# Finer loads, quartered scores, TensorE dummies and new step weights in the opening of a banded-attention and PReLU kernel

## The chip, the cores and the metric

The kernel runs on one core of one Trainium2 chip. The metric is the time of one execution on the device in microseconds (us). The core has a matrix engine, TensorE (PE in the profile, with its weight loads as PEld), three engines for elementwise work, VectorE (DVE), ScalarE (ACT) and GpSimd (POOL), and SyncE (SP), which here issues nearly all transfers between the device memory and the core's own memory. Every engine works through its own queue of instructions in a fixed order. TensorE writes its results into banks of an accumulator memory, which POOL's instructions in this kernel never touch.

## What is computed

The reference is attention over a sliding window of 64 positions, followed by a feed-forward layer whose activation is a PReLU with a slope per hidden unit (8 batches, 8 heads, 576 positions, head dimension 64; 4608 tokens, model width 512, hidden width 2048).

```python
scores = scale * np.matmul(q, k.transpose(0, 1, 3, 2))
rel = pos[:, None] - pos[None, :]
mask = (rel >= 0) & (rel < 64)
scores = np.where(mask, scores, -1000000000.0)
scores = scores - np.max(scores, axis=-1, keepdims=True)
attn = np.exp(scores)
attn = attn / (np.sum(attn, axis=-1, keepdims=True) + 1e-09)
x = np.matmul(attn, v)          # heads side by side: 4608 x 512
h = x @ w_in
g = np.maximum(h, 0.0) + alpha * np.minimum(h, 0.0)
out = (g @ w_out).astype(np.float32)
```

q, k and v are float32. The two weight matrices arrive as float64 and are taken apart inside the kernel.

## The kernel before

**Tiles.** The 4608 tokens are 36 tiles of 128. For a tile t the attention needs the queries of its two 64-position blocks and the keys and values of three blocks (its own two and the one before), with a window of 128 keys per query block. `q_load`, `k_load` and `v_load` bring them: q in one transfer of 256 KB, k in one of 384 KB (three blocks, into one of two buffers), v in two of 256 KB, each into 64 of the 128 partitions.

**Attention of a tile.** `a_score` multiplies q with k in 32 small products into two accumulator banks; the half x of the heads (even or odd head pair) has a bank each. `a_least` (DVE) adds the mask and takes the least negated score of a head, `a_exp` (ACT) the exponential with its sum, `a_sum` (ACT) adds the small constant, `a_inverse` (DVE) the reciprocal, `a_scale` (POOL) multiplies. `a_turn` transposes on PE with an identity matrix, four heads per bank, `a_turned` copies back (DVE for tiles 0 and 1, ACT after), and `a_value` multiplies with v in 32 small products. The result is split into a high part `xh` (ACT, `a_xh`) and a remainder `xl` (DVE, `a_xl`), so that two fast products stand for one exact one.

**Weights.** Each of 32 weight chunks c (even c of w_in, odd c of w_out) is a `raw` transfer of 512 KB, and runs through a chain: `tw` and `mn` (DVE) mask exponent and mantissa, `tx` (ACT) and for odd c `mx` (ACT, which puts a sign in), `ep` and `vl` (DVE) join the pieces, `pr` (POOL) multiplies, `hi` (ACT) rounds to the high part, `lo` (POOL) takes the remainder.

**Feed-forward.** A cell (n, f) is a block n of two or three tiles and a chunk f of 128 hidden units: 12 products into `h` (`m_hidden`: three pairs of high and low parts, four each), `m_slopes` (ACT) and `m_larger` (DVE) for the PReLU, `m_high` (ACT) for `gh`, `m_low` (POOL) for `gl`, and three products of 512 columns per tile into the output accumulator (`m_add`: gl with wout_h, gh with wout_l, gh with wout_h).

**Order.** The first nine tiles' attention, all weight chunks and the first three blocks (two tiles each) form the opening. `opening_graph` (L38) lists its steps with an engine, an assumed duration and what each takes and frees; `list_schedule` (L137) places them by rank (longest path plus a weight from `favour`), and the order that it draws is written out as the fixed order of each engine's queue. The names in the graph are those above: s scores, le, ex, sm, rc, sc softmax, tu transposes, td copy back, av values, xh, xl, h products, sl, la, gh, gl activation, o output products, ev and out eviction and store. A step name with `i.` ahead is the issue of a transfer. After the opening a plain loop follows (`cell`, `eighth`): one attention eighth after every few cells, with k and q of the next tile asked for at its first eighth, v at its last.

Of the kernel before, what the change touches and what calls it, by code (L numbers as in the profile page):

```python
# [18 lines left out]
RING = 6  # L19
# [6 lines left out]
WHOLE = (0, 1, 2)  # L26
# [4 lines left out]
class Op:  # L31
    def __init__(self, engine, busy, done, after, take, free):
        self.engine, self.busy, self.done = engine, busy, done
        self.after, self.take, self.free = after, take, free
        self.rank = 0.0


def opening_graph():  # L38
# [9 lines left out]
    def load(name, service, after=(), take=(), queue="SP"):  # L48
        op("i." + name, queue, 0.64, after, [take] * bool(take) + [("lane " + name, ["lane"])])
        op(name, "DMA", service, ["i." + name], free=["lane " + name])  # L50
# [6 lines left out]
    for t in range(EARLY + 1):  # L57
        done = [f"s.{t-2}.0", f"s.{t-2}.1"] if t > 1 else []
        load(f"q.{t}", 1.05, done, queue="ACT" if t == 0 else "SP")
        load(f"k.{t}", 1.6, done)  # L60
        for u in range(2):
            load(f"v.{t}.{u}", 1.05, [f"av.{t-2}"] if t > 1 else [])
    for c in range(2 * NCELL):
        load(f"raw.{c}", 2.0 if c % 2 else 2.2, take=(f"raw.{c}", ["raw"]))

    for t in attention:
        bank = ["po", "psa"] if t < 2 else ["psa"]
        score = [f"k.{t}", f"q.{t}"]
        score += ([f"s.{t-1}.0", f"s.{t-1}.1"] if t else []) + ([f"av.{t-2}"] if t > 1 else [])
        if t in WHOLE:  # L70
            op(f"s.{t}.0", "PE", 0.94, score, take=[(f"s.{t}.0", bank), (f"s.{t}.1", bank)])
            op(f"s.{t}.1", "PE", 0.0, [f"s.{t}.0"], done=0.0)
        for u in range(2):
            if t not in WHOLE:
                op(f"s.{t}.{u}", "PE", 0.87, score, take=(f"s.{t}.{u}", bank))
            for e in range(NH_PAIRS):
                g = u * NH_PAIRS + e
                op(f"le.{t}.{g}", "DVE", 0.21,
                   [f"s.{t}.{u}"] + ([f"tu.{t-2}.0", f"tu.{t-2}.1"] if t > 1 else []) + (["le.%d.0" % t] if g else []),
                   free=[f"s.{t}.{u}"] if e == NH_PAIRS - 1 else [], done=0.36)  # L80
                op(f"ex.{t}.{g}", "ACT", 0.39, [f"le.{t}.{g}"], done=0.6)
            op(f"sm.{t}.{u}", "ACT", 0.25, [f"ex.{t}.{u*NH_PAIRS+e}" for e in range(NH_PAIRS)], done=0.35)
# [3 lines left out]
            op(f"td.{t}.{u}", "ACT" if t > 1 else "DVE", 0.55 if t > 1 else 0.6,  # L86
               [f"tu.{t}.{u}"] + ([f"av.{t-2}"] if t > 1 else []), free=[f"tu.{t}.{u}"])
        op(f"av.{t}", "PE", 1.0, [f"td.{t}.0", f"td.{t}.1", f"v.{t}.0", f"v.{t}.1"]
           + ([f"h.{(t-RING)//2}.{last}"] if t >= RING else []), take=(f"av.{t}", bank))
# [23 lines left out]
    for n in range(3):  # L113
        pair = [2 * n, 2 * n + 1]
        for f in range(NCELL):
            before = [f"h.{n}.{f-1}"] if f else [f"h.{n-2}.{last}"] if n > 1 else []
            op(f"h.{n}.{f}", "PE", 1.44, [f"lo.{2*f}"] + [f"xl.{t}" for t in pair] + before,
               take=(f"h.{n}.{f}", ["ph"]))
            op(f"sl.{n}.{f}", "ACT", 0.39, [f"h.{n}.{f}", "ad"], take=(f"g.{n}.{f}", ["g"]))
# [17 lines left out]
def list_schedule(ops, slots, favour):  # L137


    names = list(ops)  # L140
    needs = {n: len(set(ops[n].after)) for n in names}
# [15 lines left out]
    for n in names:  # L157
        if not needs[n]:
            heappush(ready[ops[n].engine], (0.0 if ops[n].engine == "DMA" else -rank[n], n))
    order, begun, ends, now = [], {}, [], 0.0  # L160
    stir = set(ENGINES)
    while True:
        for e in ENGINES:
# [3 lines left out]
            while ready[e]:  # L167
                key = heappop(ready[e])
                n = key[1]
# [13 lines left out]
                heappush(ends, (now + o.busy, 0, n))  # L183
                heappush(ends, (now + o.done, 1, n))
# [7 lines left out]
        while ends and ends[0][0] <= now + 1e-9:  # L192
            _, landed, n = heappop(ends)
            if not landed:
# [5 lines left out]
            for m in then[n]:  # L200
                needs[m] -= 1
                if not needs[m]:
                    e = ops[m].engine
                    stir.add(e)
                    heappush(ready[e], (now if e == "DMA" else -rank[m], m))
    if len(order) < len(names):
        raise RuntimeError(str((now, left, [k for k, p in held.items() if p == "psa"][-6:], [n for n, _ in order[-40:]], {e: [k[1] for k in ready[e]][:8] for e in ENGINES})))
# [3 lines left out]
TILE_FAVOUR = [305, -52, 78, 372, -192, -315, -70, -391, 34, -311, -259]  # L211
BLOCK_FAVOUR = [539, 231, 26, -322]
KIND_FAVOUR = dict(
    ad=(187, -89), alpha=(6, -97), at=(-83, -32), av=(-85, 87), ep=(74, -136), ev=(86, 17), ex=(73, -346),
    gh=(-67, -185), gl=(200, 42), h=(-47, 98), hi=(71, 217), k=(142, -346), la=(-135, 6), le=(48, 49),
    lo=(68, -161), mn=(4, 37), mx=(140, 10), o=(-83, -90), out=(-109, 157), pr=(-10, -70), q=(180, 254),
    raw=(-11, 76), rc=(-89, 63), s=(-133, -145), sc=(-87, -25), sl=(92, -147), sm=(305, -95), td=(-67, 59),
    tu=(4, 120), tw=(-109, 125), tx=(117, 189), v=(-105, 115), vl=(103, -99), xh=(-25, -155),
    xl=(-104, 41),
# [3 lines left out]
def favour(name):  # L223
# [3 lines left out]
    fixed, slope = KIND_FAVOUR.get(kind, (0, 0))  # L227
    if kind in ("o", "ev", "out"):
        return BLOCK_FAVOUR[at[0] // 2] + fixed + slope * (at[1] / NCELL if kind == "o" else 1)
    if kind in ("h", "sl", "la", "gh", "gl"):  # L230
        return BLOCK_FAVOUR[at[0]] + fixed + slope * at[1] / NCELL
    if kind in ("raw", "tw", "tx", "mn", "mx", "ep", "vl", "pr", "hi", "lo"):
        return fixed + slope * at[0] / (2 * NCELL)
    if at:
        return TILE_FAVOUR[at[0]] + fixed + slope * at[0] / EARLY
    return fixed
# [3 lines left out]
def banded_attention_then_prelu_ffn(  # L240
# [41 lines left out]

    masks = const.tile([P, 3, KW], F32, name="masks")
# [42 lines left out]

    def fetch(c):
# [17 lines left out]
    def exponent(c):  # L345
        two = cv[c]["two"]
        nc.scalar.activation(two, two, AF.Relu, scale=8.0, bias=ebias if c % 2 else ebias20)
# [7 lines left out]
    def signed_mantissa(c):  # L355
        man = cv[c]["man"]
# [9 lines left out]
    def join(c):  # L366
        d = cv[c]
        d["val"] = val = io.tile([P, E], F32, tag="val", name=f"val_{c}", bufs=2)
        nc.vector.scalar_tensor_tensor(out=val, in0=d["low"],  # L369
                                       scalar=s52_sb[:, c // 2:c // 2 + 1] if c % 2 else 2.0**-32,  # L370
                                       in1=d["man"], op0=ALU.mult, op1=ALU.add)

    def product(c):
        d = cv[c]
        nc.gpsimd.tensor_tensor(out=d["val"], in0=d["val"], in1=d["exp"].bitcast(F32), op=ALU.mult)  # L375
# [8 lines left out]
    def high_part(c):  # L384
        val, hi, _ = parts(c)
        nc.scalar.copy(hi, val)

    def low_part(c):
        val, hi, lo = parts(c)
        nc.gpsimd.tensor_tensor(out=lo, in0=val, in1=hi.bitcast(F32), op=ALU.subtract)  # L390
# [7 lines left out]

    def of_tile(t, name, shape):
# [20 lines left out]
    def a_score(t, halves=(0, 1), banks=("psa", "psa")):  # L420
# [3 lines left out]
        k = d["k"].rearrange("p a (b h w) -> p a b h w", b=3, h=2)  # L424
        s = d.setdefault("s", {})
        for x, from_ in zip(halves, banks):
            s[x] = a_bank(f"s_{t}_{x}", from_)
        for a in range(2):
            for h in range(2):
                for u in range(2):  # L430
                    for x in halves:
                        r, us = slice(x * D, (x + 1) * D), slice(u * W, (u + 1) * W)
                        nc.tensor.matmul(s[x][us, 2 * a + h], q[r, a, h, us], k[r, a, u:u + 2, h, :],  # L433
# [24 lines left out]
    def a_sum(t, halves=(0, 1)):  # L458

        d = st[t]  # L460
        g = slice(halves[0] * NP, (halves[-1] + 1) * NP)
        nc.scalar.activation(d["sm"][:, g], d["sm"][:, g], AF.Identity, bias=eps)

    def a_inverse(t, halves=(0, 1)):
        d = st[t]
        g = slice(halves[0] * NP, (halves[-1] + 1) * NP)
        nc.vector.reciprocal(d["rc"][:, g], d["sm"][:, g])  # L467

    def a_scale(t, halves=(0, 1)):
        d = st[t]  # L470
        g = slice(halves[0] * NP, (halves[-1] + 1) * NP)
        w, rc = d["w"][:, g, :], d["rc"][:, g]
# [287 lines left out]
```

## Time and profile before

| | us |
|---|---|
| median of 3 runs (lowest, highest) | 934.24 (934.04, 935.03) |
| the profiled execution | 934.54 |
| its span | 932.8 |
| TensorE busy in the span | 912.3 |
| VectorE, ScalarE, GpSimd busy | 438.0, 430.5, 348.1 |

The span runs from the first to the last instruction of the program; the difference to the execution's own time lies around it. Rows of the profile name a line of the kernel (L433), the engine, the operation and the tiles as output<-input. A row of the timeline begins with start and duration; what stands in brackets is how long the engine was idle before and what ended that. A row of a group has the count, then busy time, mean duration of one in ns, and idle time before it with its causes. A wait row has total, times and longest.

### The profile page before, as it was taken

How to read it: one execution, taken by the hardware profiler on the slowest of the kernel's cores; microseconds unless marked ns; L12 is line 12 of the kernel's file. 1: busy time of each engine (PE TensorE's matmuls, PEld its weight loads, DVE VectorE, ACT ScalarE, POOL GpSimd, SP SyncE). 2: the span in 40 equal slices, each digit the busy share in tenths (PEclk: the TensorE clock that was granted, in tenths of full speed). 3: DMA queues.
4: the chain of work that ended last, by engine and by line, in shares of the span. 5: the costliest groups of instructions: out<-in, count | busy, mean ns of one | idle time of the engine just before them, and what ended most of it. 6: DMA issues, size and time to landing. Idle time of an engine off the chain costs nothing.

```text
span 932.8 us, 17053 instructions
## 1 busy us (share of the span) xinstructions
PE 912.3 (98%) x6601; PEld 812.3 (87%) x6601; DVE 438.0 (47%) x1329; ACT 430.5 (46%) x1204; POOL 348.1 (37%) x330
## 2 busy tenths in 40 slices
PE   4899999999999999999999999999999999999998
PEld 3688889888988888888889889888888888889997
DVE  5798981224544444444444444444443443443111
ACT  5887884454444434434444444444443443432322
POOL 3889994224222233333222232332322222222221
PEclk9999999999999999999999999999999999999999
DMA  9775641111322112211122112222112212100000
GB/s 254 212 207 176 192 147 46 52 54 45 102 52 85 51 52 66 55 51 52 52 53 85 51 52 86 51 52 85 52 51 55 83 51 52 57 1 1 34 1 34
DMA packets 55216, 69.78 MB, mean 75 GB/s; under 512 B 3408, under 2 KB 48480, under 8 KB 55136
## 3 DMA queue, kind: packets, MB, share of 16 engines
q1 hardware_dynamic: 54832, 68.43, 26.0%
q8 instruction: 52, 0.85, 0.4%
q10 hardware_dynamic: 304, 0.27, 0.1%
q14 instruction: 28, 0.23, 0.1%
HBM read 59.25 MB, written 9.44 MB: 74 GB/s over the span
## 4 chain that ended last, share of the span: by engine, by line
PE 94%; DVE 2%; POOL 2%; ACT 1%; DMA 1%; issue 0%; POOLq 0%; DVEq 0%
PE h L565 43%; PE o L608 42%; PE s L433 4%; PE av L507 4%; PE t L490 1%; ACT w L451 1%; POOL val L375 1%; DMA q<-qT 1%; POOL w L473 0%; POOL gl L594 0%; POOL wout_l L390 0%; POOL win_l L390 0%; DVE exp L363 0%; DVE val L369 0%; DVE two L342 0%
## 5 line engine op out<-in xcount | busy, mean ns | idle before, releaser
L594 POOL TENSOR_TENSOR gl<-g,gh 128x384 fp32r<-128x384 f32 (+1 forms) x208 | 197.3, 948 | 548.9 <-ACT gh L587 543.3
L580 DVE SCALAR_TENSOR_TENSOR g<-h,s_sb,g 128x384 f32<-128x384 f32 (+1 forms) x208 | 122.0, 587 | 336.4 <-ACT g L574 333.6
L574 ACT ACTIVATE g<-h,sa_sb 128x384 f32<-128x384 f32 (+1 forms) x208 | 115.6, 556 | 262.7 <-PE h L565 258.4
L608 PE MATMUL o<-wout_h,gl 128*128 128x512 f32 x576 | 227.6, 395 | 1.2 <-POOL gl L594 1.2
L608 PE MATMUL o<-wout_l,gh 128*128 128x512 f32 x576 | 226.9, 394 | 0.0
L608 PE MATMUL o<-wout_h,gh 128*128 128x512 f32 x576 | 224.2, 389 | 0.0
L565 PE MATMUL h<-xh,win_h 128*128 128x384 f32 (+1 forms) x832 | 174.2, 331 | 0.4 <-DVE g L580 0.3
L565 PE MATMUL h<-xl,win_h 128*128 128x384 f32 (+1 forms) x832 | 168.8, 324 | 0.0
L565 PE MATMUL h<-xh,win_l 128*128 128x384 f32 (+1 forms) x832 | 167.8, 323 | 0.0
L587 ACT CAST gh<-g 128x384 fp32r<-128x384 f32 (+1 forms) x208 | 101.6, 489 | 124.4 <-DVE g L580 118.6
L565 PEld LDWEIGHTS h<-xh,win_h 128*128 128x128 f32 x832 | 141.3, 188 | 18.8 <-issue 1.2
L485 DVE STREAM_TRANSPOSE pt<-w 32x256 f32<-32x256 f32 x324 | 141.2, 436 | 5.5
L565 PEld LDWEIGHTS h<-xl,win_h 128*128 128x128 f32 x832 | 142.4, 188 | 0.1
L565 PEld LDWEIGHTS h<-xh,win_l 128*128 128x128 f32 x832 | 139.6, 188 | 0.0
L608 PEld LDWEIGHTS o<-wout_h,gh 128*128 128x128 f32 x576 | 108.1, 188 | 24.2
L451 ACT ACTIVATE w<-w,nm 128x128 f32<-128x128 f32 x288 | 113.1, 396 | 28.0 <-DVE nm L444 27.7
L608 PEld LDWEIGHTS o<-wout_h,gl 128*128 128x128 f32 x576 | 108.1, 188 | 18.5 <-POOL gl L594 1.8
L608 PEld LDWEIGHTS o<-wout_l,gh 128*128 128x128 f32 x576 | 108.3, 188 | 13.5
L444 DVE CUSTOM_DVE_ANT_0 w<-s,masks 128x128 f32<-128x128 f32 x288 | 71.1, 285 | 15.6 <-PE s L433 15.3
L473 POOL TENSOR_TENSOR w<-w,rc 128x1024 f32<-128x1024 f32 (+1 forms) x45 | 70.0, 1558 | 18.8 <-DVE rc L467 18.8
L518 DVE TENSOR_TENSOR xl<-av,xh 128x512 fp32r<-128x512 f32 x36 | 24.9, 691 | 99.6 <-ACT xh L513 99.5
L433 PEld LDWEIGHTS s<-k,q 64*64 64x64 f32 x1152 | 39.4, 142 | 24.0 <-PE o L608 9.6
(46 smaller groups left out, 535.1 us busy)
## 6 DMA issues: line engine op xcount, KB each, us to landing
v<-vN SPq DMA_DIRECT2D x72, 256.0 KB, 4.2
k<-kT SPq DMA_DIRECT2D x36, 384.0 KB, 4.7
out<-os SPq DMA_DIRECT2D x36, 256.0 KB, 2.3
q<-qT SPq DMA_DIRECT2D x35, 256.0 KB, 4.3
raw<-w_in SPq DMA_DIRECT2D x16, 512.0 KB, 4.1
raw<-w_out SPq DMA_DIRECT2D x16, 512.0 KB, 3.6
q<-qT ACTq DMA_DIRECT2D x1, 256.0 KB, 5.2
alpha_rows<-alpha ACTq DMA_DIRECT2D x1, 8.0 KB, 5.0
```

The source lines that it names most:

```text
L433: nc.tensor.matmul(s[x][us, 2 * a + h], q[r, a, h, us], k[r, a, u:u + 2, h, :], start=True, stop=True)
L444: nc.vector.tensor_tensor_reduce(out=d["w"][:, g, :], in0=d["s"][u][:, e], in1=mask, op0=ALU.add, op1=ALU.min, scale=-SCALE, scalar=3.0e38 ...
L451: nc.scalar.activation(w, w, AF.Exp, scale=-1.0, bias=d["nm"][:, g:g + 1], accum_out=d["sm"][:, g:g + 1])
L473: nc.gpsimd.tensor_tensor(out=w, in0=w, in1=rc.unsqueeze(2).broadcast_to(list(w.shape)), op=ALU.mult)
L485: nc.vector.transpose(pt[ks, :, r], w[r, :, ks])
L507: nc.tensor.matmul(av[r, e, us], v[:, e, u, r], pt[:, g, us], start=True, stop=True)
L565: nc.tensor.matmul(ph[:, :nt], wt[:, c, fs], xt[:, c, xs], start=(k == 0), stop=(k == 3 * NP - 1))
L574: nc.scalar.activation(g, ph[:, :nt], AF.Copy, scale=sa_sb[:, f:f + 1])
L580: nc.vector.scalar_tensor_tensor(out=g, in0=ph[:, :nt], scalar=s_sb[:, f:f + 1], in1=g, op0=ALU.mult, op1=ALU.max)
L587: nc.scalar.copy(gh, gs[n, f])
L594: nc.gpsimd.tensor_tensor(out=gl, in0=g, in1=gh.bitcast(F32), op=ALU.subtract)
L608: nc.tensor.matmul(po[t], gt[:, ts], wt[:, f, :], start=(f == 0 and k == 0), stop=(f == NF - 1 and k == 2))
```

## The change

It has these parts; the first three hold for all 36 tiles and all cells, the others for the opening alone:

1. v is loaded in four transfers of 128 KB per tile, one for each head pair, each into all 128 partitions. The source pattern is written by hand: two overlapping pairs of blocks, 64 positions, 256 elements.
2. k lives in a ring of seven blocks over three tiles: the first tile of a round loads three blocks (384 KB), the other two load two (256 KB).
3. In `m_add` the three products come in the order gh with wout_h, gl with wout_h, gh with wout_l (also after the opening).
4. Tile 0's q and k are loaded in two parts each (a).
5. For tiles 0, 1, 5, 6, 7 and 8 the score step is cut by a, not by bank: a step fills two quarters of both banks, and the softmax, transposes and copies of a half go with it (`heads`, `of_half`).
6. The identity is made on POOL ahead of the masks, and 40 products of the identity with itself stand in PE's queue as dummies of lowest rank.
7. The first three cells' products of each opening block become three steps each, with needs of their own.
8. 43 steps move to DVE: 19 gl, 5 lo, 6 pr, 7 sc from POOL, 3 td and 3 xh from ACT; the copies td of tiles 0 and 1 go from DVE to ACT. For the one odd chunk whose lo moves, mx falls away and the sign comes in with hi and lo.
9. Assumed durations and the rank weights are new, so the fixed order of all queues in the opening is drawn anew.

```diff
+COUPLED = (0, 1, 5, 6, 7, 8)
+APART = (0,)
+WARM = 40
+FINE = 3
+KRING = 3
+MOVED = (
+    "gl.0.1", "gl.0.5", "gl.0.6", "gl.0.8", "gl.0.10", "gl.0.14", "gl.1.1", "gl.1.3", "gl.1.6", "gl.1.8",
+    "gl.1.9", "gl.1.13", "gl.1.15", "gl.2.0", "gl.2.6", "gl.2.7", "gl.2.9", "gl.2.11", "gl.2.13", "lo.4",
+    "lo.8", "lo.9", "lo.24", "lo.26", "pr.5", "pr.11", "pr.27", "pr.28", "pr.29", "pr.30", "sc.4.1",
+    "sc.5.0", "sc.6.0", "sc.6.1", "sc.7.0", "sc.7.1", "sc.8.1", "td.2.1", "td.7.0", "td.8.0", "xh.2",
+    "xh.6", "xh.7",
+)
...
+def heads(t, u):
+
+    if t in COUPLED:
+        return [2 * u, 2 * u + 1, NH_PAIRS + 2 * u, NH_PAIRS + 2 * u + 1]
+    return list(range(u * NH_PAIRS, (u + 1) * NH_PAIRS))
...
-        load(f"k.{t}", 1.6, done)
-        for u in range(2):
-            load(f"v.{t}.{u}", 1.05, [f"av.{t-2}"] if t > 1 else [])
+            load(f"k.{t}" + f".{a}" * (a != ""), (1.2 if t % KRING == 0 else 0.8) * part, done)
+        for e in range(NH_PAIRS):
+            load(f"v.{t}.{e}", 0.42, [f"av.{t-2}"] if t > 1 else [])
     for c in range(2 * NCELL):
-        load(f"raw.{c}", 2.0 if c % 2 else 2.2, take=(f"raw.{c}", ["raw"]))
+        load(f"raw.{c}", 1.6 if c % 2 else 1.65, take=(f"raw.{c}", ["raw"]))
+
+    for i in range(WARM):
+        op(f"wm.{i}", "PE", 1.35 if i == 0 else 0.45 if i < 8 else 0.3, [f"wm.{i-1}"] if i else [], take=("wm", ["po"]) if not i else (),
+           free=["wm"] if i == WARM - 1 else [])
...
+    for name in MOVED:
+        kind, *at = name.split(".")
+        to, busy = {"td": ("DVE", 0.6), "xh": ("DVE", 0.6), "gl": ("DVE", 0.35)}.get(kind, ("DVE", 0.62))
+        o = ops[name]
+        o.engine, o.busy, o.done = to, busy, busy + 0.12
...
-    def k_load(t):
-        nc.sync.dma_start(of_tile(t, "k", [P, 2, 6 * W]),
-                          kT[:, :, 2 * t:2 * t + 3].rearrange("(a x) d b h w -> (x d) a (b h w)", x=2))
-
-    def v_load(t, u):
-        nc.sync.dma_start(of_tile(t, "v", [P, NP, 2, P])[u * W:(u + 1) * W].rearrange("w c b d -> w c (b d)"),
-                          vN[:, :, 2 * t + u:2 * t + u + 2].rearrange("c w b d -> w c (b d)"))
+    def k_load(t, a=None):
+        at = 2 * (t % KRING)
+        new = 1 if at else 0
+        part = slice(0, 2) if a is None else slice(a, a + 1)
+        from_ = kT[:, :, 2 * t + new:2 * t + 3].rearrange("(a x) d b h w -> (x d) a (b h w)", x=2)
+        nc.sync.dma_start(kring[:, part, at + new:at + 3].rearrange("p a b h w -> p a (b h w)"), from_[:, part])
+
+    def v_load(t, e):
+        (_, _), w, b, d = vN.ap
+        blocks_from = vN[e, :, 2 * t:2 * t + 2].offset
+        nc.sync.dma_start(of_tile(t, "v", [P, NP, 2, P])[:, e].rearrange("p b d -> p (b d)"),
+                          bass.AP(vN.tensor, blocks_from, [list(b[:1]) + [2], list(w), [d[0], 2 * P]]))
...
-        for k, (gt, wt) in enumerate(((gl, wout_h), (gh, wout_l), (gh, wout_h))):
-            nc.tensor.matmul(po[t], gt[:, ts], wt[:, f, :],
+        for k in parts:
+            of_g, wt = (("gh", wout_h), ("gl", wout_h), ("gh", wout_l))[k]
+            nc.tensor.matmul(po[t], g[of_g][:, ts], wt[:, f, :],
...
+    def warm(i):
+        if i == 0:
+            cv["warm"] = ps_o.tile([P, E], F32, tag="po", name="warm")
+        nc.tensor.matmul(cv["warm"][:, :P], ident, ident, start=True, stop=True)
```

More of the change, by code (lines that the diff above doesn't have):

```diff
@@ L58, in opening_graph @@
         done = [f"s.{t-2}.0", f"s.{t-2}.1"] if t > 1 else []
-        load(f"q.{t}", 1.05, done, queue="ACT" if t == 0 else "SP")
-        load(f"k.{t}", 1.6, done)
-        for u in range(2):
-            load(f"v.{t}.{u}", 1.05, [f"av.{t-2}"] if t > 1 else [])
-    for c in range(2 * NCELL):
-        load(f"raw.{c}", 2.0 if c % 2 else 2.2, take=(f"raw.{c}", ["raw"]))
+        for a in range(2) if t in APART else ("",):
+            part = 0.5 if t in APART else 1.0
+            load(f"q.{t}" + f".{a}" * (a != ""), 0.8 * part, done, queue="ACT" if t == 0 else "SP")
+            load(f"k.{t}" + f".{a}" * (a != ""), (1.2 if t % KRING == 0 else 0.8) * part, done)
@@ L67, in opening_graph @@
         bank = ["po", "psa"] if t < 2 else ["psa"]
[L68 to L72, printed above, removed]
-        for u in range(2):
[L74 to L77, printed above, removed]
+        before = ([f"s.{t-1}.0", f"s.{t-1}.1"] if t else []) + ([f"av.{t-2}"] if t > 1 else [])
@@ new lines, in opening_graph @@
+        for u in range(2):
+            loaded = [f"{x}.{t}.{u}" if t in APART else f"{x}.{t}" for x in "qk"]
+            if t not in COUPLED:
+                op(f"s.{t}.{u}", "PE", 0.87, loaded + before, take=(f"s.{t}.{u}", bank))
+            elif u == 0:
+                op(f"s.{t}.0", "PE", 0.5, loaded + before, take=[(f"s.{t}.0", bank), (f"s.{t}.1", bank)])
+            else:
+                op(f"s.{t}.1", "PE", 0.47, loaded + [f"s.{t}.0"])
+        for u in range(2):
+            for g in heads(t, u):
+                x, e = divmod(g, NH_PAIRS)
@@ L85, in opening_graph @@
             op(f"tu.{t}.{u}", "PE", 0.44, [f"sc.{t}.{u}"], take=(f"tu.{t}.{u}", bank))
[L86 removed]
+            op(f"td.{t}.{u}", "ACT", 0.55,
                [f"tu.{t}.{u}"] + ([f"av.{t-2}"] if t > 1 else []), free=[f"tu.{t}.{u}"])
[L88 to L89 removed]
+        op(f"av.{t}", "PE", 1.0, [f"td.{t}.0", f"td.{t}.1", *(f"v.{t}.{e}" for e in range(NH_PAIRS))]
+           + ([f"h.{(t-RING)//2}.{last}.2"] if t >= RING else []), take=(f"av.{t}", bank))
         op(f"xh.{t}", "ACT", 0.5, [f"av.{t}"])
@@ L158, in list_schedule @@
         if not needs[n]:
-            heappush(ready[ops[n].engine], (0.0 if ops[n].engine == "DMA" else -rank[n], n))
+            heappush(ready[ops[n].engine], (0.0 if ops[n].engine == "DMA" else -rank[n], at[n]))
     order, begun, ends, now = [], {}, [], 0.0
@@ L182, in list_schedule @@
                 order.append((n, got))
-                heappush(ends, (now + o.busy, 0, n))
-                heappush(ends, (now + o.done, 1, n))
+                heappush(ends, (now + o.busy, 2 * key[1]))
+                heappush(ends, (now + o.done, 2 * key[1] + 1))
                 break
@@ L204, in list_schedule @@
                     stir.add(e)
-                    heappush(ready[e], (now if e == "DMA" else -rank[m], m))
+                    heappush(ready[e], (now if e == "DMA" else -rank[m], at[m]))
     if len(order) < len(names):
-        raise RuntimeError(str((now, left, [k for k, p in held.items() if p == "psa"][-6:], [n for n, _ in order[-40:]], {e: [k[1] for k in ready[e]][:8] for e in ENGINES})))
+        raise RuntimeError("the opening stops short")
     return order, begun
-TILE_FAVOUR = [305, -52, 78, 372, -192, -315, -70, -391, 34, -311, -259]
-BLOCK_FAVOUR = [539, 231, 26, -322]
+TILE_FAVOUR = [-64, -249, 807, 675, -762, -455, -933, -821, -494, -1277, -742]
+BLOCK_FAVOUR = [46, 778, 1029, 0]
 KIND_FAVOUR = dict(
[L214 to L219, printed above, removed]
+    ad=(407, 253, -534), alpha=(331, 236, 115), at=(-391, 185, 499), av=(-187, -108, 48), ep=(156, 0, 86),
+    ev=(183, -53, -60), ex=(-105, 122, -53), gh=(-256, 103, -64), gl=(351, 299, 7), h=(140, -397, -150),
+    hi=(-142, -244, 160), k=(-65, -406, -157), la=(304, 367, -109), le=(-361, 463, 106),
+    lo=(-227, -75, 241), mn=(28, -172, 190), mx=(-251, -411, 19), o=(-488, 66, 204), out=(-318, 16, 217),
+    pr=(66, 352, 32), q=(338, 853, 128), raw=(-275, -89, -212), rc=(416, 217, -146), s=(343, -632, -43),
+    sc=(32, -137, 9), sl=(-145, -21, 49), sm=(172, 30, -84), td=(-71, -393, -205), tu=(-216, 372, -114),
+    tw=(61, 38, -337), tx=(-37, -399, 92), v=(-625, 538, 169), vl=(300, -337, -319), xh=(149, -589, -21),
+    xl=(789, -288, -104),
 )
@@ L280, in banded_attention_then_prelu_ffn @@
     ps_a = ctx.enter_context(tc.tile_pool(name="ps_a", bufs=3, space=PSUM))
+    ident = const.tile([P, P], F32, name="ident")
+    nc.gpsimd.memset(ident, 1.0)
+    nc.gpsimd.affine_select(out=ident, in_=ident, compare_op=ALU.is_equal, fill=0.0,
+                            base=0, pattern=[[-1, P]], channel_multiplier=1)
     masks = const.tile([P, 3, KW], F32, name="masks")
@@ L325, in banded_attention_then_prelu_ffn, with on, late_sign @@
     cv = {}
+    graph = opening_graph()
+    def on(name):
+        return {"POOL": nc.gpsimd, "DVE": nc.vector}[graph[name].engine if name in graph else "POOL"]
+    def late_sign(c):
+        return c % 2 == 1 and graph[f"lo.{c}"].engine == "DVE"
     def fetch(c):
@@ L346, in exponent @@
         two = cv[c]["two"]
-        nc.scalar.activation(two, two, AF.Relu, scale=8.0, bias=ebias if c % 2 else ebias20)
+        nc.scalar.activation(two, two, AF.Relu, scale=8.0, bias=ebias if c % 2 and not late_sign(c) else ebias20)
     def mask_mantissa(c):
@@ L374, in product @@
         d = cv[c]
-        nc.gpsimd.tensor_tensor(out=d["val"], in0=d["val"], in1=d["exp"].bitcast(F32), op=ALU.mult)
+        on(f"pr.{c}").tensor_tensor(out=d["val"], in0=d["val"], in1=d["exp"].bitcast(F32), op=ALU.mult)
     def parts(c):
@@ L488, in a_turn @@
         st[t].setdefault("tp", {})[u] = tp = a_bank(f"t_{t}_{u}", from_)
-        for e in range(NP):
-            nc.tensor.transpose(tp[:, e], st[t]["w"][:, u * NP + e, :], ident)
+        for e, g in enumerate(heads(t, u)):
+            nc.tensor.transpose(tp[:, e], st[t]["w"][:, g, :], ident)
     def a_turned(t, u):
-        pt = pts[t % 2][:, u * NP:(u + 1) * NP, :]
-        if t < 2:
-            nc.vector.tensor_copy(pt, st[t]["tp"][u])
+        tp, pt = st[t]["tp"][u], of_half(t, pts[t % 2], u)
+        if len(pt.shape) == 4:
+            tp = tp.rearrange("p (x h) k -> p x h k", x=2)
+        if graph[f"td.{t}.{u}"].engine == "DVE":
+            nc.vector.tensor_copy(pt, tp)
         else:
-            nc.scalar.copy(pt, st[t]["tp"][u])
+            nc.scalar.copy(pt, tp)
     def a_value(t, from_="psa"):
@@ L512, in a_xh @@
         xs = slice((place[n] + i) * P, (place[n] + i + 1) * P)
-        nc.scalar.copy(xh[:, :, xs], st[t]["av"])
+        if f"xh.{t}" in graph and graph[f"xh.{t}"].engine == "DVE":
+            nc.vector.tensor_copy(xh[:, :, xs], st[t]["av"])
+        else:
+            nc.scalar.copy(xh[:, :, xs], st[t]["av"])
     def a_xl(t):
@@ L550, in eighth, with m_hidden @@
             if t + 1 < NT:
-                v_load(t + 1, 0)
-                v_load(t + 1, 1)
+                for e in range(NP):
+                    v_load(t + 1, e)
     gs = {}
-    def m_hidden(n, f):
+    def m_hidden(n, f, parts=(0, 1, 2)):
         nt = len(blocks[n]) * P
@@ L560, in m_hidden @@
         xs = slice(place[n] * P, (place[n] + len(blocks[n])) * P)
-        ph = ps_h.tile([P, 512], F32, tag="ph", name=f"h_{n}_{f}")
-        k = 0
-        for wt, xt in ((win_h, xh), (win_h, xl), (win_l, xh)):
+        if 0 in parts:
+            gs[n, f] = ps_h.tile([P, 512], F32, tag="ph", name=f"h_{n}_{f}")
+        for k in parts:
+            wt, xt = ((win_h, xh), (win_h, xl), (win_l, xh))[k]
             for c in range(NP):
-                nc.tensor.matmul(ph[:, :nt], wt[:, c, fs], xt[:, c, xs],
-                                 start=(k == 0), stop=(k == 3 * NP - 1))
-                k += 1
-        gs[n, f] = ph
+                nc.tensor.matmul(gs[n, f][:, :nt], wt[:, c, fs], xt[:, c, xs],
+                                 start=(k == 0 and c == 0), stop=(k == 2 and c == NP - 1))
     def m_slopes(n, f):
```

190 lines of the change are left out of this document (114 added, 76 removed).

## The prediction

> **What bounds the kernel now.** I read the page first, then the busy time by stretches, then PE's waits, and last the rows of the first 70 us.
>
> ```profile
> span 932.8 us, 17053 instructions
> PE 912.3 (98%) x6601; PEld 812.3 (87%) x6601; DVE 438.0 (47%) x1329; ACT 430.5 (46%) x1204; POOL 348.1 (37%) x330
> ```
>
> TensorE (PE) is busy for 912.3 of 932.8 us, so only 20.5 us are idle. The next answer, columns stretch, length, PE busy, clock, DMA, says where they lie.
>
> ```profile
> 0.00:68.29 68.29, 51.47 (x495) 1.00 0.82 223
> 68.29:920.00 851.71, 851.71 (x6065) 1.00 0.22 63
> 920.00:932.80 12.80, 9.10 (x43) 1.00 0.17 61
> ```
>
> From 68.29 to 920 us PE never stops. The tail idles 3.70 us behind the last matmul. The other 16.82 us lie before 68.29, in the planned opening. The change leaves PE's useful work as it is (same products, same counts), so the time can fall only by those 16.82 us and by PE instructions that ran slowly there; it can rise wherever PE is starved anew. PE's waits up to 70 us (total, times, longest):
>
> ```profile
> PE s L433 <- DMA q<-qT: 6.1, 1, 6.1
> PE t L490 <- POOL w L473: 3.4, 3, 1.6
> PE s L433 <- DVE nm L444: 2.0, 1, 2.0
> PE s L433 <- DVE val L369: 1.9, 2, 1.2
> PE o L608 <- POOL gl L594: 1.2, 2, 1.0
> ```
>
> After the first load, no wait of PE ends on a DMA: softmax and weight conversion end them.
>
> **The change part by part.** The span is that of one execution of 934.54 us (1.74 us lie around it); the median is 934.24, 0.30 less. I sum against 934.54 and take 0.30 off.
>
> ```profile
> 6.06 1.98 PE L433 MATMUL s<-k,q 64*64 64x128 f32 x32 [6.06 <-DMA q<-qT]
> ...
> 12.71 1.12 PE L490 MATMUL t<-ident,w 128*128 128x128 f32 x4 [0.34 <-POOL w L473]
> ...
> 15.71 0.70 PE L507 MATMUL av<-pt,v 128*64 128x64 f32 x8
> 16.57 1.55 PE L507 MATMUL av<-pt,v 128*64 128x64 f32 x24 [0.16 <-DVE pt L495]
> ...
> 34.38 1.13 PE L490 MATMUL t<-ident,w 128*128 128x128 f32 x8
> ...
> 41.61 1.15 PE L507 MATMUL av<-pt,v 128*64 128x64 f32 x32
> ```
>
> ```profile
> q<-qT ACTq DMA_DIRECT2D x1, 256.0 KB, 5.2
> ...
> DMA packets 6315, 7.74 MB, mean 258 GB/s; under 512 B 352, under 2 KB 6000, under 8 KB 6312
> ```
>
> *Tile 0's q and k in two parts each.* The first scores then need 128 + 192 KB instead of 256 + 384. At the 258 GB/s of the first 30 us the 320 KB left out are 1.2 us of the 5.2 from issue to landing. Bounds: 0 (the second part lands as late as now and the softmax waits for it) to 2.5 us. I take -1.3, with the earlier identity and scores in it.
>
> *Quarters.* A score step becomes 16 matmuls over two banks instead of 32, so tile 0's and tile 1's first softmax can start half of 1.98 us earlier. In each tile the chain later meets the other half. Bounds 0 to 2; I take -1.0.
>
> *Dummies.* Forty 128-column matmuls on the identity, which is now made first on POOL. The same shape cost 1.12 us for four at 12.71 and 1.13 for eight at 34.38, so one is 0.14 to 0.28 us and all are 5.6 to 11.2 us. Some 3 us of them fit before the first score; the rest stand in PE's fixed order among the 10 us of gaps up to 40 us. A dummy waits for nothing, so in a true gap it costs nothing; where work is ready it costs 0.14 to 0.28. I take +0.5, bounds 0 to +3 (ten of them in the way). What they may bring: four early transposes take 1.12, half of the eight at 34.38 0.56; the first values 0.70 + 1.55 = 2.25 against 1.15 at 41.61. On the path of tiles 0 and 1 stand one such transpose and one value step each: 2 x (0.5 + 1.1) = 3.2 us. Bounds 0 to -3.2; I take -2.0, because gaps stay between the steps. The granted clock is 1.00 in every stretch, so it is the durations that show this, not that column. By the Trainium skill (TensorE: Matmul & The Clock Gate, Part 1: The HAM clock gate) the array runs at half rate until about 3.4 us of sustained work, and falls back after as long an idle window. By that rule the gaps of 2 us need no filling, and the gain would be the whole 3.2; the durations agree with the halving, the granted clock does not show it.
>
> *v and k loads.* Two loads of v alone (170 to 173 us), then q with k (183.8 to 186.5):
>
> ```profile
> DMA packets 544, 0.52 MB, mean 175 GB/s; under 512 B 32, under 2 KB 544, under 8 KB 544
> ...
> q1 hardware_dynamic: 544, 0.52, 75.7%
> ```
>
> ```profile
> DMA packets 544, 0.66 MB, mean 243 GB/s; under 512 B 32, under 2 KB 544, under 8 KB 544
> ...
> q1 hardware_dynamic: 544, 0.66, 73.9%
> ```
>
> The old v goes to 64 partitions: 75.7% of 3.0 us is 2.27 us of all 16 engines for 0.52 MB. q and k go to 128: 73.9% of 2.7 is 2.0 us for 0.66 MB, 3.05 us per MB. At that rate a tile's v takes 1.6 us, 0.7 less. The ring spares 128 KB of k in two tiles of three, 0.4 us each. Over the first 30 us (three v, four spared k) that is 3.7 us of a queue that is nearly full. But no PE wait after the first ends on it, so I take -0.5, bounds 0 to -3.7; the other end, for quarters that load slower than that, is a rival below. Each tile issues six loads instead of four, at 0.4 to 0.6 us of SP each; in the steady part that is 3.6 us in some 25 us, and SP queues nothing that waits for it. The ring adds waits of k.t behind scores of earlier tiles; scores of t-2 already held the load before. If the whole ring counts as one buffer, k.t waits for s.t-1, and the next raw loads behind it on SP with it.
>
> *Finer first products, gh first.* PE waits 1.2 us for gl. The high part is there a POOL subtraction earlier (0.744 us), so -0.7, bounds 0 to -1.2.
>
> *Moved steps.* POOL loses 19 gl, 5 lo, 6 pr, 7 sc; ACT loses 3 td and 3 xh; DVE takes these 43 and gives the four td of tiles 0 and 1 to ACT.
>
> ```profile
> L375 POOL TENSOR_TENSOR val<-val,exp 128x512 f32<-128x512 f32 x32 | 41.4, 1297 | 8.4 <-DVE val L369 8.4
> L594 POOL TENSOR_TENSOR gl<-g,gh 128x256 fp32r<-128x256 f32 x30 | 22.3, 744 | 2.0 <-ACT gh L587 2.0
> ...
> L473 POOL TENSOR_TENSOR w<-w,rc 128x512 f32<-128x512 f32 x13 | 13.6, 1050 | 12.0 <-DVE rc L467 12.0
> ```
>
> ```profile
> L580 DVE SCALAR_TENSOR_TENSOR g<-h,s_sb,g 128x256 f32<-128x256 f32 x30 | 14.4, 481 | 3.9 <-ACT g L574 3.8
> ...
> L518 DVE TENSOR_TENSOR xl<-av,xh 128x512 fp32r<-128x512 f32 x6 | 4.1, 685 | 0.8 <-ACT xh L513 0.7
> ```
>
> ```profile
> 30.00:68.00 38.00, 36.03 (x324) 30.26 (x322) 33.41 (x95) 32.58 (x93) 31.60 (x31) 1.00 0.69 197
> 68.00:140.00 72.00, 71.71 (x548) 62.52 (x548) 64.38 (x147) 57.62 (x144) 69.72 (x67) 1.00 0.57 174
> ```
>
> POOL is relieved of 19 x 0.744 + 11 x 1.30 + 7 x 1.05 = 35.8 us. DVE takes 19 x 0.48 + 24 x 0.69 = 25.7 and gives 4 x 0.69 = 2.8: +22.9. Between 68 and 140 us (columns PE, PEld, DVE, ACT, POOL) POOL is full, yet PE does not wait: three blocks wait for it. So the relief is worth nothing there, and I count 0. Its cover is PE's backlog; gone, DVE is late (a rival).
>
> **The sum:** -1.3 - 1.0 + 0.5 - 2.0 - 0.5 - 0.7 = -5.0; 934.54 - 5.0 - 0.30 = **929.2 us**. The remaining waits (POOL w, DVE nm, DVE val) hang on an order that the new step weights draw anew; I count them as they are. Adding the terms' ends: at best -12.4, at worst +3; not all ends come together, so 924 to 933 is the forecast's own range.
>
> **The rivals.**
>
> *The v quarters load on few engines (slower).* A quarter's source pattern counts 2 first (blocks), then 64 (positions), where the old one counts 64 first. If a transfer is dealt to the engines by its outermost count, a quarter runs on 2 of 16. For: nothing in the trace speaks against it, since every transfer there has an outermost count of 16 or more and so could be dealt to 16. Against: all of those do run on 16 (32 packets under 512 B for two v loads, 16 completions each), and no row has a smaller spread. Price: 64 KB on each of two engines; q and k move 0.66 MB in 2.0 us on 16, 20.5 GB/s each, so 3.2 us a quarter and 12.8 us a tile on the same two engines, in front of every later load of the queue. Four tiles are 51 us of those engines, where the second block's products begin at 48.26 us now and need tiles 0 to 3:
>
> ```profile
> 48.26 0.74 PE L565 MATMUL h<-xh,win_h 128*128 128x256 f32 x4
> ```
>
> With q, k and eight raw loads in between (about 16 us at the same rate) they would begin near 70 us, and the weights behind them would be late by 15 to 45 us. PE drinks that up in part; +30 over the forecast, 945 to 985, **960 us**. The steady part would hold: 12.8 + 3 us of the two engines in some 25 us per tile. The point of decision: it costs as soon as a v load stands ahead of a raw load that PE is short of. The Trainium skill (DMA: Bandwidth & Descriptors, Why a DMA increments its semaphore by 16 and not by 1) states just this rule: the largest count up to 16 that divides both patterns' slowest dimension. No run here shows it yet. Chance **0.32**.
>
> *The gain is eaten (no change).* DVE, 64.38 of 72 us busy between 68 and 140, gets 22.9 us more, and the conversion ends some 10 us later; or the reordered first tiles wait as long as now elsewhere. Against it: 35.8 us less on POOL, and PE's backlog. 932.5 to 936, **934**. Chance **0.10**.
>
> *Dummies and early rows in the way (slower).* All bounds at their poor end: thirty dummies at 0.28 in front of ready work are 8 us, less 5. **937 us**, deciding once more than some twenty stand in the way. Against: the gaps are 10 us wide. Chance **0.06**.
>
> **How the numbers follow.** The forecast has 0.52 of the chance. Faster by over 0.2% (1.9 us, about what a measurement of this kernel can tell from no change): 0.52. Within 0.2%: 0.10. Slower: 0.32 + 0.06 = 0.38. The range goes from 924 to 965: it leaves out little below and about half of the first rival above, some 0.18 in all. Cases of both signs hold the chance, so the likeliest one's own range, 924 to 933, stands beside it.
>
> **What would show it.** The first score row before 5 us (start); four transposes at 0.6 us before 15 us (dummies); PE's wait for gl gone (products); v alone at 1.6 us of engine time per tile, landings near 4 us (loads); PE unbroken from before 68 us; DVE over 9 tenths and POOL under 8 between 68 and 140 us. Wrong: packets under 512 B of two per v quarter instead of 16, v landing after 6 us or more, the value step or raw's readers waiting for a DMA, and PE idle between 20 and 100 us. That would be the first rival.

## The result: slower by 7.9%

The changed kernel takes 1008.22 us (four runs, 1006.31 to 1009.18) against 934.14 us before. The ratio is 1.079, with a 95% interval from 1.0771 to 1.081. The forecast was 929.2 us; the first rival, to which the prediction gave 0.32, has the right sign and the right mechanism, but its 945 to 985 us (960) end below the time that came.

The page of the changed kernel, the lines that answer to those of before:

```profile
span 1004.6 us, 17274 instructions
...
PE 940.6 (94%) x6681; PEld 834.7 (83%) x6681; DVE 461.3 (46%) x1368; ACT 429.4 (43%) x1201; POOL 317.4 (32%) x293
...
PEclk9658898999999999999999999999999999999999
DMA  5335443311211212121211211211211211200000
...
DMA packets 54385, 66.64 MB, mean 66 GB/s; under 512 B 2576, under 2 KB 47648, under 8 KB 54304
```

The DMA row of the page before:

```profile
DMA  9775641111322112211122112222112212100000
```

Of the 71.8 us that the span has grown, 43.5 are idle time of TensorE (64.0 us against 20.5) and 28.3 are busy time. The PEclk and DMA rows are fortieths of the span, in tenths: the clock granted to TensorE is at 5 to 9 tenths between 25 and 175 us, and the DMA engines, at 9 to 4 tenths in the first 140 us before, are at 5 to 3 in the first 175 us now. The packets under 512 B count the completions: before, they are 3408 for 213 transfers, 16 each. Now, of the 287 transfers, 143 are not v; at 16 each they make 2288, and the 288 that are left are **two for each of the 144 quarters of v**. So a quarter runs on two engines, and the others are not short of work, but stand idle while these two are overrun. From 30 to 44 us, with one raw chunk and five quarters of v issued, the row of the engines is this (fortieths of the 14 us), at some 45 GB/s wherever it shows one tenth:

```profile
DMA  1111111111111457999411111111111111111111
```

Busy time by stretch of the changed kernel (columns: length, PE, PEld, DVE, ACT, POOL, granted clock, DMA share, GB/s):

```profile
0.00:30.00 30.00, 23.82 (x212) 20.09 (x213) 14.60 (x72) 16.29 (x60) 12.81 (x21) 0.85 0.53 172
30.00:68.00 38.00, 21.64 (x169) 17.69 (x169) 14.98 (x42) 12.75 (x38) 11.59 (x10) 0.59 0.33 105
68.00:140.00 72.00, 54.12 (x384) 46.08 (x384) 49.96 (x114) 39.90 (x103) 34.83 (x33) 0.88 0.41 125
140.00:200.00 60.00, 44.50 (x277) 37.95 (x277) 42.20 (x73) 30.12 (x59) 30.68 (x28) 0.89 0.41 127
...
300.00:900.00 600.00, 596.18 (x4269) 535.78 (x4266) 274.76 (x879) 250.37 (x732) 175.87 (x154) 1.00 0.18 56
```

PE is idle for 6.2, 16.4, 17.9 and 15.5 us in the first four stretches, 55.9 of the 64.0. From 30 to 68 us every engine is busy for four to six tenths of its time before, as it would be if all lacked data. The plain loop (300 to 900) loses 3.8 us, in one wait for k.

Where the data is, SP's own queue shows (start, duration of the issue):

```profile
4.79 8.97 SPq L499 DMA_DIRECT2D v<-vN  x4
13.89 2.73 SPq L487 DMA_DIRECT2D q<-qT  x1
...
22.90 3.38 SPq L400 DMA_DIRECT2D raw<-w_out  x1
26.32 3.99 SPq L499 DMA_DIRECT2D v<-vN  x2
30.41 3.65 SPq L400 DMA_DIRECT2D raw<-w_in  x1
34.16 10.15 SPq L499 DMA_DIRECT2D v<-vN  x4
44.40 3.20 SPq L487 DMA_DIRECT2D q<-qT  x1
```

Issuing one v transfer of before held SP for 0.6 us. In the first 72 us it now holds SP for 1.9 to 2.9 us in the mean of a group, and the q or raw next behind it for 2.7 to 3.7. That fits a queue that cannot hand out more pieces until the two engines have taken some; no run tests this by itself. What TensorE then waits for most, up to 200 us:

```profile
PE h L660 <- DVE exp L432: 16.9, 4, 8.0
PE h L660 <- DVE g L673: 15.1, 5, 7.9
PE av L598 <- DMA v<-vN: 9.1, 4, 3.0
PE t L579 <- DVE pt L586: 6.1, 1, 6.1
```

Only 9.1 us are put down to v itself. The larger waits name VectorE, but it was busy for only 15.0 of the 38 us from 30 to 68 and 50.0 of the 72 after: they end on VectorE steps that themselves come late, behind raw chunks behind v in SP's queue. The idle time of VectorE before a step that reads raw shows it (total, times):

```profile
  DMA raw<-w_out: 37.8, 6
  DMA raw<-w_in: 17.4, 3
```

These are 55.2 us; in the kernel before there is no such wait, and in the run e2 below 0.8 us. The page's chain of work that ended last names raw too, and so do the pieces of that chain (start, duration):

```profile
PE h L660 38%; PE o L702 36%; DMA raw<-w_out 5%; PE s L519 4%; PE av L598 4%; SPq L499 2%; DMA v<-vN 1%; DMA raw<-w_in 1%; DVE two L409 1%; DVE exp L432 1%; DMA k<-kT 1%; DVE man L419 1%; DVE val L439 1%; DVE g L673 1%; PE t L579 1%
```

```profile
30.41 11.22 DMA raw<-w_in
...
94.41 10.94 DMA raw<-w_out
```

Six raw transfers, of 8.4 to 11.2 us from issue to landing, make 60.5 us of the chain; before, the median was 4.1 us for w_in and 3.6 for w_out. The raw of 30.41 us shows two causes: it holds SP for 3.65 us, the engines then move most of it from 34.6 to 37.0 us, and it has landed only at 41.63, after a stretch at one tenth. How the loss divides between the held queue and the pieces on the two engines is not shown.

### The profile page after: what moved, and what is told of

Same layout as the page of the kernel before. It is cut to its first block, busy times and chain, and to the rows that moved or that the text cites. A ratio compares the mean times of both kernels' runs of the same rounds, so it can differ in the third digit from the quotient of the medians.

```text
span 1004.6 us, 17274 instructions
## 1 busy us (share of the span) xinstructions
PE 940.6 (94%) x6681; PEld 834.7 (83%) x6681; DVE 461.3 (46%) x1368; ACT 429.4 (43%) x1201; POOL 317.4 (32%) x293
## 3 DMA queue, kind: packets, MB, share of 16 engines
q1 hardware_dynamic: 53984, 65.28, 20.5%
## 4 chain that ended last, share of the span: by engine, by line
PE 82%; DMA 8%; DVE 5%; SPq 3%; ACT 1%; issue 1%; ACTq 0%; DVEq 0%
PE h L660 38%; PE o L702 36%; DMA raw<-w_out 5%; PE s L519 4%; PE av L598 4%; SPq L499 2%; DMA v<-vN 1%; DMA raw<-w_in 1%; DVE two L409 1%; DVE exp L432 1%; DMA k<-kT 1%; DVE man L419 1%; DVE val L439 1%; DVE g L673 1%; PE t L579 1%
## 5 line engine op out<-in xcount | busy, mean ns | idle before, releaser
L687 POOL TENSOR_TENSOR gl<-g,gh 128x384 fp32r<-128x384 f32 (+1 forms) x189 | 183.9, 973 | 580.4 <-ACT gh L680 572.6
L702 PE MATMUL o<-wout_h,gh 128*128 128x512 f32 x576 | 227.6, 396 | 0.0
L660 PE MATMUL h<-xh,win_h 128*128 128x384 f32 (+1 forms) x832 | 178.6, 337 | 32.8 <-DVE exp L432 16.9
L660 PEld LDWEIGHTS h<-xh,win_h 128*128 128x128 f32 x832 | 143.9, 193 | 54.4 <-DVE g L673 18.8
L660 PE MATMUL h<-xl,win_h 128*128 128x384 f32 (+1 forms) x832 | 171.7, 328 | 0.1
L660 PEld LDWEIGHTS h<-xl,win_h 128*128 128x128 f32 x832 | 145.5, 192 | 1.6 <-DVE xl L612 0.4
L562 POOL TENSOR_TENSOR w<-w,rc 128x1024 f32<-128x1024 f32 (+1 forms) x38 | 63.2, 1665 | 43.0 <-DVE rc L558 43.0
L519 PE MATMUL s<-k,q 64*64 64x128 f32 x1152 | 50.0, 295 | 5.3 <-DMA k<-kT 3.8
```

The source lines that it names most:

```text
L519: nc.tensor.matmul(s[x][us, 2 * a + h], q[r, a, h, us], kring[r, a, at + u:at + u + 2, h, :], start=True, stop=True)
L562: on(f"sc.{t}.{u}").tensor_tensor(out=w, in0=w, in1=rc.unsqueeze(len(rc.shape)).broadcast_to(list(w.shape)), op=ALU.mult)
L660: nc.tensor.matmul(gs[n, f][:, :nt], wt[:, c, fs], xt[:, c, xs], start=(k == 0 and c == 0), stop=(k == 2 and c == NP - 1))
L687: on(f"gl.{n}.{f}").tensor_tensor(out=gl, in0=g, in1=gh.bitcast(F32), op=ALU.subtract)
L702: nc.tensor.matmul(po[t], g[of_g][:, ts], wt[:, f, :], start=(f == 0 and k == 0), stop=(f == NF - 1 and k == 2))
```

## The experiments

All runs keep the reference's computation. In the runs that lay v out anew, the array handed to the kernel holds each row of a tile with its two blocks side by side (1 KB), so that 128 rows of 1 KB follow each other.

**Quarters back to halves, the order kept** (e1):

```diff
-        nc.sync.dma_start(of_tile(t, "v", ...)[:, e]..., bass.AP(..., [list(b[:1]) + [2], list(w), [d[0], 2 * P]]))
+        if e < 2:
+            nc.sync.dma_start(of_tile(t, "v", ...)[e * W:(e + 1) * W]..., vN[:, :, 2 * t + e:2 * t + e + 2]...)
```

> The changed kernel in all but v, which comes again in two transfers per tile into 64 partitions each, issued where the first two quarters stood; the fixed order of every other instruction is that of the changed kernel. Theory A (the quarters run on two DMA engines, and that is the whole loss): 925 to 935 us, packets under 512 B back to 16 per transfer, PE idle before 70 us below 17 us. Theory B (the new order, the dummies or DVE's 43 extra steps starve PE): it stays above 970 us. Between: both have a part.

941.45 us, 1.0071 of before (1.0056 to 1.0086): 67 of the 74 us are gone with v alone. It lies between the two theories, above the 925 to 935 of A: on the new order the old loads of v still cost 6.4 us more than the quarters of the next run.

**The same four transfers, 128 rows counted first** (e2):

```diff
-                          bass.AP(vN.tensor, blocks_from, [list(b[:1]) + [2], list(w), [d[0], 2 * P]]))
+                          vN[e, t])        # 128 rows of 256 elements
```

> The changed kernel with the same four transfers of 128 KB per tile into 128 partitions and the same queue order, but v laid out in device memory so that the source pattern counts 128 rows first (each row holds its two blocks, 1 KB). Theory A: the number of engines follows the outermost count, so 16 completions per quarter, a quarter lands in some 2.5 us, and the time is 924 to 933 us. Rival C (a small transfer into 128 partitions is slow in itself, or four issues per tile are): above 960 us.

935.07 us, 1.0007 (0.9997 to 1.0016). Size, number, destination and order of the transfers are those of the changed kernel; the count that stands first in the pattern differs, and 73.2 us go with it. The rows also lie side by side in device memory now; they do so (but for a spare row after each 32) in the run with four counted first, below, too, and that one still loses. Its page:

```profile
DMA packets 56401, 66.65 MB, mean 71 GB/s; under 512 B 4592, under 2 KB 49664, under 8 KB 56320
...
v<-vN SPq DMA_DIRECT2D x144, 128.0 KB, 2.5
```

4592 is 287 x 16, and a quarter lands 2.5 us after its issue. Theory A stands. But this run is also 2 us above the upper end that I gave, and not told apart from the kernel before: the rest of the change brings nothing that can be measured.

**The quarters alone, on the kernel before** (e3: `v_load` and the plan's four names for v from the change, nothing else):

> The kernel before with v in the four quarters of the change (2 counted first) and nothing else; assumed loads of v are 0.52 us each, so the rest of the plan stays nearly as it was. Theory A: slower by 40 to 90 us, 975 to 1025 us, with PE idle in the opening and a lower granted clock there. Theory B: below 945 us.

1008.99 us, 1.0794 (1.0778 to 1.081): the whole loss from this one part with its plan, and with 0.60 of the clock granted between 30 and 68 us. Theory B falls.

```profile
30.00:68.00 38.00, 17.64 (x189) 14.90 (x188) 19.09 (x73) 16.30 (x54) 17.23 (x15) 0.60 0.39 120
```

**The quarters from tile 10 on only** (e4):

```diff
+        if t > EARLY:
             nc.sync.dma_start(...)          # the quarter, 2 counted first
+        elif e < 2:
+            nc.sync.dma_start(...)          # the old half
```

> The changed kernel with old halves of v for tiles 0 to 9 and the quarters (2 counted first) from tile 10 on, in the plain loop. Theory A with the opening as its place: within 6 us above the run with halves throughout (the loop has slack: 12.8 + 3 us of two engines in some 25 us a tile), 928 to 941 us. If the loop itself is short of the two engines: above 950 us.

945.55 us, 4.1 us above the run with halves throughout; the absolute range is missed because that run came out higher. One wait of TensorE for k (4.1 us, at 256 us, early in the plain loop) is all of it. In the loop two engines carry v beside the rest, as this window of the changed kernel shows (a tile's four quarters issued at 243.72; fortieths of 13 us):

```profile
DMA  4699996220101111111111111111111111448999
GB/s 79 205 359 333 366 369 199 71 63 32 44 28 38 47 47 50 47 47 50 47 44 44 44 44 44 44 44 44 44 44 47 47 44 44 117 132 274 362 340 325
```

After q and k (first eight fields) some 8 us run at one tenth of the engines and 44 to 47 GB/s: two engines at 22 to 23 GB/s each. A tile's 512 KB take some 11.5 us so.

**Four counted first** (e8: the changed kernel with v laid out in four groups of 32 rows, a spare row after each):

> The changed kernel, same transfers, with v laid out so that the pattern counts 4 first, then 32 rows. Theory A (as many engines as the outermost count): 4 completions per quarter, half the time of a quarter on twice the engines, so 5.8 us of four engines per tile instead of 11.6 of two; the loss shrinks to less than half of the 74 us, 940 to 965 us. If the number of engines were either 2 or 16 only: 1000 us or 935 us.

959.17 us, 1.0262 (1.0249 to 1.0276). Its page:

```profile
DMA packets 54673, 66.65 MB, mean 70 GB/s; under 512 B 2864, under 2 KB 47936, under 8 KB 54592
```

2864 is 2288 + 144 x 4: four engines per quarter. The loss over the run with 16 is 24.1 us, a third of that with two. So the number of engines follows the first count, and the time follows the number of engines.

The next runs ask why the rest of the change, freed of this, gives 0 instead of the -5 of the forecast. Stretches and waits of e2:

```profile
0.00:30.00 30.00, 24.67 (x285) 20.96 (x287) 21.42 (x87) 21.37 (x73) 19.47 (x27) 0.94 0.83 267
30.00:68.00 38.00, 35.89 (x326) 29.66 (x323) 35.86 (x105) 30.23 (x95) 21.96 (x21) 1.00 0.61 191
68.00:140.00 72.00, 68.01 (x487) 56.56 (x486) 69.41 (x132) 50.68 (x109) 51.67 (x45) 1.00 0.50 152
```

```profile
PE h L657 <- DVE g L670: 3.4, 4, 1.0
PE t L576 <- POOL w L559: 2.1, 3, 1.3
PE warm L764 <- POOL ident L344: 1.8, 1, 1.8
PE h L657 <- DVE exp L432: 1.4, 2, 1.1
```

Between 68 and 140 us VectorE is full (69.4 of 72 us), GpSimd has 20 us to spare, and PE, which before idled 0.29 us there, idles 3.99, for `g` and `exp` from VectorE.

**Without dummies** (e5, e2 with `warm` emitting nothing):

> The kernel with v counted by 128 rows first (935.07 us), without the 40 dummies; the order of everything else stays. If they fill true gaps and speed up what follows (my term: +0.5 - 2.0): 935.5 to 938 us, with the early transposes at 1.1 us for four again. If they stand in the way by about as much as they bring: within 0.7 us of 935.07. If they are in the way: 931 to 934 us.

937.51 us, 1.0028 (1.0017 to 1.0039), 2.4 above e2 (2.0 by the two ratios to before). The rows show how; e5, then e2:

```profile
13.66 1.11 PE L576 MATMUL t<-ident,w 128*128 128x128 f32 x4 [2.50 <-POOL w L559]
15.05 1.12 PE L576 MATMUL t<-ident,w 128*128 128x128 f32 x4 [0.28 <-POOL w L559]
```

```profile
5.55 0.86 PE L516 MATMUL s<-k,q 64*64 64x128 f32 x16
...
12.67 0.66 PE L576 MATMUL t<-ident,w 128*128 128x128 f32 x4 [0.52 <-POOL w L559]
...
31.48 0.74 PE L657 MATMUL h<-xh,win_h 128*128 128x256 f32 x4
```

The dummies are worth what they cost and 2 us or a little more. They also hold up the first score, which begins at 4.87 us without them and at 5.55 with them.

**gl back on GpSimd** (e6, e2 with the 19 moved `gl` on POOL, same order):

```diff
+        here = name in graph and not name.startswith("gl.")
-        return {...}[graph[name].engine if name in graph else "POOL"]
+        return {...}[graph[name].engine if here else "POOL"]
```

> The kernel with v counted by 128 rows first, with the 19 moved gl back on POOL in the same order of steps; 12 lo, pr, sc each less or more are not touched. If DVE (69.4 of 72 us busy between 68 and 140 us, PE idle 4.0 us there behind it) ate the gain: DVE loses some 19 x 0.45 = 8.6 us, PE's idle time there falls below 1.5 us, 932 to 933.5 us. If DVE's load is not the cause: 934.5 to 937 us.

932.43 us, 0.9977 (0.9967 to 0.9987): 2.6 below e2 and below the kernel before.

```profile
68.00:140.00 72.00, 69.93 (x508) 59.18 (x508) 66.03 (x126) 52.77 (x116) 59.09 (x57) 1.00 0.48 147
```

VectorE falls by 3.4 us in this stretch and PE's idle time from 3.99 to 2.07, not to the 1.5 expected.

**pr and lo back too** (e10, but for the one lo with the late sign):

> The run with gl back on POOL (932.43 us), with pr and all lo but the one with the late sign back on POOL too, in the same order. If DVE's load is still what PE waits for: 931 to 932 us, DVE below 63 of 72 us between 68 and 140. If POOL, at 59 of 72 us there, fills up and becomes the wait: 933 to 936 us.

933.01 us, 0.9986 (0.9977 to 0.9995), not told apart from e6. VectorE comes down to 61.85 us in the stretch, GpSimd up to 66.93, and PE's idle time is 3.04: it now waits 2.1 us for gl on GpSimd. The relief of one engine is the load of the other. (The profile of e10 is of its longest execution, 935.35 us, that of e6 of its shortest, 931.25, so their idle times may show more difference than there is.)

**Two v transfers of 256 KB instead of four** (e11, on e6):

> The run with gl back on POOL (932.43 us), with v in two transfers of 256 KB per tile at the places of the first and third, 128 rows counted first. If four issues per tile hold SP's queue up in the opening: 931 to 932.2 us. If not: within 0.7 us of 932.43.

931.8 us, 0.9972 (0.9961 to 0.9983), the fastest of the series, though its runs (931.25 to 933.24) overlap those of e6. It fits both expectations, so whether four issues per tile cost anything stays open.

**The new v on the order of before** (e7, four transfers per tile; e9, two of 256 KB, no step of the order changed):

> The kernel before with v in four 128 KB transfers per tile whose pattern counts 128 rows first; nothing else of the change but the assumed 0.52 us per v transfer. My term for v: -0.3 to 0 of the -0.5, so 933.5 to 934.5 us. If v's slower transfers into 64 partitions held the opening up: 929 to 932 us. If four issues are a burden on SP: 935 to 938 us.

> The kernel before, its fixed order unchanged step for step, with v laid out in rows and its two transfers per tile of 256 KB each going into 128 partitions (128 rows counted first). It parts the faster transfer from the order that four names per tile draw. If the 939.64 us of the four-transfer run came from its redrawn order: 933 to 934.5 us, v landing below 4 us. If v into 128 partitions hurts in itself: 937 us or more. If faster v loads are worth the 0.7 us of queue time per tile: 931 to 933 us.

e7: 939.64 us, 1.0049 (1.0037 to 1.0061). e9: 935.48 us, 1.0003 (0.9993 to 1.0012). e7 is 4 to 5 us worse than e9 and the kernel before. The waits speak for the order that four names for v draw in the plan (in e7 PE waits 9.9 us for `w` on POOL, against 3.9 in e9), but four issues stand there in place of two as well, and no run parts these. v's faster transfer by itself (e9) is worth nothing that can be measured on this order. e7 and e3 have one plan: 1008.99 - 939.64 = 69.4 us is the price of two engines on the order of before, 73.2 on the new one.

## Why the prediction was wrong

**The step that failed** stands under "v and k loads": "At that rate a tile's v takes 1.6 us, 0.7 less." The rate was that of q and k, whose patterns count 128 rows first; v's new pattern counts 2 blocks first. I took the nearest row and let the number of partitions, not the order of the pattern, decide what is near. Measured: some 11.5 us a tile on two engines, and 73.2 us of time where I had -0.5 for loads. The rule that I put among the rivals, that a transfer is dealt to the engines by its outermost count, was right: e2, e8 and the change itself count 128, 4 and 2 first and have 16, 4 and 2 completions per quarter, and 935, 959 and 1008 us. The Trainium skill (DMA: Bandwidth & Descriptors, Why a DMA increments its semaphore by 16 and not by 1) states it, for both patterns of a transfer; the three runs, which vary the source's count alone, agree. For want of a row in the trace of before with fewer than 16, I gave it 0.32.

**The rival's price was mis-sized.** "+30 over the forecast" became 79 over it, and 73.2 over e2. The time of a tile was near (12.8 us forecast, some 11.5 shown). Too small was what it does to the loads behind it: I counted the first four tiles' v in front of the second block, had the weights late "by 15 to 45 us", and wrote that PE "drinks that up in part". But eight tiles' v go through SP's queue up to 167 us, with raw chunks in between; VectorE waits 55.2 us for raw, and PE, with 43.5 us more of idle time, drinks up little of it. And PE, starved, then ran slower: between 30 and 68 us a product of 256 columns took 456 to 470 ns in the mean, against 282 to 299 before.

```profile
L660 PE MATMUL h<-xh,win_h 128*128 128x256 f32 x8 | 2.4, 456 | 0.0
```

```profile
L565 PE MATMUL h<-xh,win_h 128*128 128x256 f32 x36 | 6.4, 299 | 0.1
```

The first fence is the changed kernel, the second the one before, both from 30 to 68 us. Of the 28.3 us more that PE is busy, 15.9 are the dummies; the other 12.4 are work that took longer than before, as these rows do.

**"The steady part would hold"** was right in kind: 4.1 us in e4.

**The other terms**, read from the runs with 16 engines, were right in sign and too hopeful in sum. Dummies: +0.5 - 2.0 = -1.5 forecast, -2.0 to -2.4 shown (e5); their length was misread, since the 40 fill 80 rows and 13.2 us in e2, not 5.6 to 11.2. gl: the wait of 1.2 us is gone from e2's list, as said. v: -0.5 for loads forecast, 0 for v shown (e9). Start: the first score at 5.55 us instead of 6.06, less than half of the 1.3, because dummies stand before it (4.87 without them), and the first product at 31.48 instead of 32.86. The moved steps were counted 0, because "PE does not wait: three blocks wait for it". That fell: in the new order VectorE is full and PE waits for it. Moving gl back gives 2.6 us (e6), so 0 should have been about +2.6. That part is the second rival, in whose range (932.5 to 936) e2 lies; its mechanism is shown for gl, while pr and lo make no difference (e10). What is left between e6 (1.8 us below the runs of before beside it) and the -5.0 is not traced to single steps: the order as a whole was redrawn, and quarters, ring and halves of q and k were not tried one by one. The terms' best ends add up to -12.6, not -12.4, which moves nothing.

Also open: how much of the 73 us would go if another queue than SP's issued the two-engine quarters. That was not tried.

## What to carry to other kernels

Before a transfer is cut anew, write down the count that stands first in its source pattern: with bytes and partitions the same, that set the number of engines here (2, 4 and 16), and the packets under 512 B in the profile tell it here (completions divided by transfers). A transfer on few engines is paid for by those behind it in the queue that issues it, and the waits then carry other names than its own. A step moved off a full engine is a gain only if the engine that takes it has room in the stretch that TensorE waits in; after such a change, look at that stretch again.

## What the runs showed of the hardware

- One transfer of 128 KB on two engines moves at 22 to 23 GB/s per engine, and in the opening holds the issuing queue for some 2 to 2.9 us (8.97 and 10.15 for four, 20.08 for seven), where a load of v before held it for 0.6.
- The granted clock fell to 0.59 (changed kernel) and 0.60 (e3) between 30 and 68 us, while PE was busy for 21.6 and 17.6 of 38 us. In the first 30 us of the kernel before it read 1.00 although PE was busy for 15.4 of 30 us and four transposes took 1.12 us at 12.71, against 0.66 at 12.67 in e2; so that column alone does not tell whether PE ran at its full pace. The Trainium skill (TensorE: Matmul & The Clock Gate, Part 1: The HAM clock gate) has half rate after an idle window; the durations agree.
- A subtraction to the rounded type, `gl` with 256 columns, took VectorE 799 ns in the mean in e2's first 140 us (12 of them), longer than a product of 512 columns (706) and than the 744 ns that GpSimd took before:

```profile
L684 DVE TENSOR_TENSOR gl<-g,gh 128x256 fp32r<-128x256 f32 x12 | 9.6, 799 | 0.1
L445 DVE TENSOR_TENSOR val<-val,exp 128x512 f32<-128x512 f32 x6 | 4.2, 706 | 0.0
```

The mean hides two kinds: the 19 of the whole run took 409 to 1429 ns with a median of 425, and the seven after 140 us, where GpSimd was busy for only 11.8 of 60 us, took 415 to 425. Whether GpSimd's work beside them makes the others long was not tested.
